# First chunk's scores of a fused attention and MoE kernel: one row for the cumulated gates against a product with a selection matrix

## The chip, the cores and the metric

The kernel runs on one core of a Trainium2 chip. The metric is the device time of one execution in microseconds (us), as the median of several runs. An engine is named PE (TensorE, matmuls), PEld (its weight loads), DVE (VectorE), ACT (ScalarE), POOL (GpSimd) or SP (SyncE, which issues most DMAs).

## What is computed

Attention with a decay from cumulated gates, then a mixture of four experts, then a gated MLP, all in float32 on 1152 tokens of width 512.

```python
B, H, S, D = 2, 8, 576, 64
scores = q @ k.T / sqrt(D)
cum = cumsum(log(clip(f, 1e-4, 1)))
scores = where(causal, -1e9, scores + cum[query] - cum[key])
x = softmax(scores) @ v
out = sum_e p[e] * (relu(x @ w1[e]) @ w2[e])
h = out @ w_in
y = (h * sigmoid(1.702 * h)) @ w_out
```

The term cum[query] is the same for all keys of a row and falls out of the softmax; only cum[key] is added.

## The kernel before

The tokens are four chunks: of each of the two batches its first 256 and its last 320. Attention is done chunk by chunk, and as soon as a chunk is ready the expert layers on it are put between the attention steps of later chunks, so that PE always has matmuls. After attention the expert and MLP layers run over three wide chunks of 384 tokens. Numbers in the layers are split in a high and a low part of type float32r, and three products of one pass each stand for one float32 product. `w_pairs` holds the weight loads, `due` and `need` say how many attention steps (`pull`) go between two layer groups, and the framework's scheduler then decides the order of each engine's instructions.

Attention goes by units. For each unit there are stages in a software pipeline: scores (PE, line 394), mask and row maximum (DVE, L420), exponential with row sum (ACT, L434), division by the sum (DVE L440 and L441, POOL L443), transposition (PE L461, copied out by ACT L53 or DVE L468), product with v (PE L491). The scores go to two buffers in PSUM (`ps_s`), so PE may write the scores of a tile only when DVE has read the tile two before it.

Chunk 0, the first 256 tokens of batch 0, is the one that `plain` names. It has no high and low parts: its score products are float32 products, which the chip runs as two passes. A unit of it is one head with two query tiles, one of 128 queries by 128 keys and one of 128 by 256. Eight heads make eight units.

For these, `load_plain` (L293) loads for four heads at a time k (`kd`) and q (`qd`) transposed, 64 partitions each, and v (`vd`). A 65th row is added: ones times 1/NEG in `qd` (a POOL memset, L304, NEG is -1/8), and the cumulated gates in `kd`, which `load_plain_rest` (L306) brings by two DMAs that ACT issues (L310) when the first half of the gates is cumulated. The product over 65 rows then holds the scores and the gates.

The gates themselves: `fr` is loaded, clipped (DVE L657), its logarithm taken (ACT L658), summed along the row (DVE L659), each in two halves of 256 and 320 columns. Then `cumd` is written to DRAM (L665, issued by ACT) for the later chunks, which read it back as rows spread over partitions (`cb`, `cbs`). For the later chunks q and k of a head pair stand on two halves of 64 partitions (`load_heads`, L320), and POOL splits them (`prep_parts`, L50 and L333).

```python
qd, kd, vd = groups[h0]
nc.scalar.dma_start(out=kd[64:65], in_=cum[h0:h0 + G, :wk])
for g in range(G):
    heads[0, h0 + g] = dict(vd=vd[:, :, g, :], qd=qd[:65, g], kd=kd[:65, g])
```

## Time and profile before

| | us |
|---|---|
| median of 3 runs | 737.25 |
| lowest and highest run | 737.0, 743.86 |
| the profiled execution | 737.77 |
| its span in the trace | 736.1 |
| PE busy | 715.6 |
| POOL busy | 277.6 |

All times in the trace count from the start of the span. The profiled execution has 1.7 us around its span. PE is busy for 97% of the span, but matmuls are pipelined, so that its records overlap; a busy PE is not a PE at its peak.

### The profile page before, as it was taken

To read this page: it belongs to the slowest core of one execution; us is meant where nothing else is said; L and a number is where in the kernel's file an instruction comes from. 1 tells how busy PE (TensorE), PEld (TensorE's weight loads), DVE (VectorE), ACT (ScalarE), POOL (GpSimd) and SP (SyncE) were. 2 spreads that over 40 slices of the span, in tenths; PEclk is the share of its full clock that TensorE was granted. 3 is DMA by queue.
4 is the path that set the end of the run, shared out by engine and by line. 5 is a ranking of instruction groups with operands and counts; after the bars stand their busy time and mean duration, and the time that the engine had idled before them with its cause. 6 is when DMAs were issued, how large, how long until landed. Compare 5 with 4: busy or idle time off the path is not lost.

```text
span 736.1 us, 11924 instructions
## 1 busy us (share of the span) xinstructions
PE 715.6 (97%) x4488; PEld 674.9 (92%) x4488; DVE 460.2 (63%) x1023; ACT 268.4 (36%) x629; POOL 277.6 (38%) x345
## 2 busy tenths in 40 slices
PE   4999999999999999999999999999999999999998
PEld 3576788888899999999998999999999999999997
DVE  4785666575758999999999633445972124424422
ACT  4564554566542233222211221223354433323420
POOL 4886974653432022233232433232462222222220
PEclk9999999999999999999999999999999999999999
DMA  8776534332216464464443301000100000000012
GB/s 290 222 233 208 159 123 132 90 103 86 73 51 216 144 194 149 148 183 117 130 144 115 86 24 35 1 1 1 58 0 1 1 1 1 1 0 1 1 44 86
DMA packets 29496, 67.23 MB, mean 91 GB/s; under 512 B 3032, under 2 KB 4576, under 8 KB 29440
## 3 DMA queue, kind: packets, MB, share of 16 engines
q1 hardware_dynamic: 29392, 66.44, 28.9%
q8 instruction: 35, 0.57, 0.3%
q14 instruction: 21, 0.17, 0.1%
q10 hardware_dynamic: 48, 0.05, 0.0%
HBM read 64.05 MB, written 2.41 MB: 90 GB/s over the span
## 4 chain that ended last, share of the span: by engine, by line
PE 75%; DVE 13%; DMA 5%; issue 3%; POOL 3%; ACT 0%; ACTq 0%; DVEq 0%; POOLq 0%
PE m L604 32%; PE m L560 31%; PE s L394 5%; PE t L461 3%; PE x L491 3%; DVE wlo L163 3%; DMA mst<-in_wa_mlp_dram 2%; DMA mst<-in_wb_mlp_dram 2%; DVE cvd L226 1%; DVE wf L220 1%; DVE cvt L214 1%; DVE tmp L618 1%; DVE cvt L212 1%; DVE hl L587 1%; DVE wf L228 1%
## 5 line engine op out<-in xcount | busy, mean ns | idle before, releaser
L620 POOL TENSOR_TENSOR acc<-acc,tmp 128x384 f32<-128x384 f32 (+3 forms) x112 | 111.2, 1004 | 248.9 <-DVE tmp L618 238.0
L604 PE MATMUL m<-hh,wlo 128*128 128x384 f32 (+2 forms) x640 | 128.0, 320 | 1.4 <-DVE wlo L163 1.3
L604 PE MATMUL m<-hh,whi 128*128 128x384 f32 (+2 forms) x640 | 129.1, 321 | 0.0
L604 PE MATMUL m<-hl,whi 128*128 128x384 f32 (+2 forms) x640 | 127.7, 320 | 0.0
L560 PE MATMUL m<-xh,whi 128*128 128x384 f32 (+2 forms) x624 | 126.1, 322 | 0.4 <-DVE hl L587 0.2
L560 PE MATMUL m<-xl,whi 128*128 128x384 f32 (+2 forms) x624 | 126.2, 321 | 0.0
L560 PE MATMUL m<-xh,wlo 128*128 128x384 f32 (+2 forms) x624 | 126.2, 321 | 0.0
L53 ACT ACTIVATE whi<-wst 128x512 fp32r<-128x512 f32 x103 | 64.9, 631 | 119.8 <-PE m L560 58.0
L163 DVE TENSOR_TENSOR wlo<-wst,whi 128x512 fp32r<-128x512 f32 x112 | 93.3, 836 | 24.3 <-ACT whi L53 13.7
L604 PEld LDWEIGHTS m<-hh,wlo 128*128 128x128 f32 x640 | 105.6, 188 | 3.2 <-DVE wlo L163 2.4
L604 PEld LDWEIGHTS m<-hh,whi 128*128 128x128 f32 x640 | 105.8, 188 | 1.7 <-issue 0.7
L560 PEld LDWEIGHTS m<-xh,whi 128*128 128x128 f32 x624 | 103.1, 188 | 3.7 <-issue 1.7
L604 PEld LDWEIGHTS m<-hl,whi 128*128 128x128 f32 x640 | 105.9, 188 | 0.8 <-issue 0.5
L560 PEld LDWEIGHTS m<-xl,whi 128*128 128x128 f32 x624 | 103.8, 188 | 0.9 <-issue 0.7
L560 PEld LDWEIGHTS m<-xh,wlo 128*128 128x128 f32 x624 | 103.7, 188 | 1.1 <-issue 1.0
L595 POOL TENSOR_TENSOR hl<-tmp,hh 128x384 fp32r<-128x384 f32 x48 | 49.1, 1025 | 133.3 <-ACT hh L53 133.3
L586 ACT ACTIVATE hh<-m 128x384 fp32r<-128x384 f32 (+2 forms) x112 | 48.9, 436 | 117.5 <-PE m L560 117.5
L587 DVE SCALAR_TENSOR_TENSOR hl<-m,hh 128x384 fp32r<-128x384 f32 (+2 forms) x112 | 54.9, 493 | 34.9 <-ACT hh L586 34.9
L618 DVE TENSOR_TENSOR tmp<-m,dpb 128x384 f32<-128x384 f32 (+2 forms) x80 | 40.9, 512 | 38.4 <-PE m L604 32.0
L593 DVE TENSOR_TENSOR tmp<-m,sg 128x384 f32<-128x384 f32 x48 | 26.6, 554 | 54.2 <-ACT sg L592 54.2
L443 POOL TENSOR_SCALAR e<-e,sm 128x128 f32<-128x128 f32 (+4 forms) x72 | 47.4, 668 | 29.4 <-DVE sm L441 15.7
L434 ACT ACTIVATE e<-e,mx 128x128 f32<-128x128 f32 (+4 forms) x72 | 41.9, 583 | 35.9 <-DVE mx L420 34.9
(80 smaller groups left out, 742.6 us busy)
## 6 DMA issues: line engine op xcount, KB each, us to landing
wst<-in_wa_moe_dram SPq DMA_DIRECT2D x28, 512.0 KB, 3.5
wst<-in_wb_moe_dram SPq DMA_DIRECT2D x28, 512.0 KB, 3.8
mst<-in_wa_mlp_dram SPq DMA_DIRECT2D x16, 512.0 KB, 3.5
mst<-in_wb_mlp_dram SPq DMA_DIRECT2D x16, 512.0 KB, 3.6
cb<-cumd SPq DMA_DIRECT2D x16, 256.0 KB, 4.1
vd<-in_vp_dram SPq DMA_DIRECT2D x8, 320.0 KB, 13.1
kq<-in_qk_dram SPq DMA_DIRECT2D x4, 608.0 KB, 7.2
cbs<-cumd SPq DMA_DIRECT2D x8, 288.0 KB
```

What stands on the lines that cost most here:

```text
L53: nc.scalar.activation(out=out, in_=in_, func=AF.Copy)
L163: sub = nc.vector.tensor_sub(lf, raw, f(hf))
L394: nc.tensor.matmul(pt[:, :z - a], lhsT=lr[i][0], rhs=lr[i][1], start=i == 0, stop=i == n - 1)
L434: nc.scalar.activation(out=e[:, off:off + w], in_=e[:, off:off + w], func=AF.Exp, scale=-1.0, bias=mx, accum_out=sm[:, 0, k:k + 1])
L443: nc.gpsimd.tensor_scalar(out=e[:, off:off + w], in0=e[:, off:off + w], scalar1=sm[:, 0, i:i + 1], scalar2=1.0, op0=ALU.mult, op1=ALU.mult)
L560: nc.tensor.matmul(p[:, :n], lhsT=w[:, k, :], rhs=x[c][:, k, :], start=(j == 0 and k == 0), stop=(j == 2 and k == 3))
L586: nc.scalar.activation(out=hh[:, g, :n], in_=p[:, :n], func=AF.Relu)
L587: nc.vector.scalar_tensor_tensor(out=hl[:, g, :n], in0=p[:, :n], scalar=0.0, in1=f(hh[:, g, :n]), op0=ALU.max, op1=ALU.subtract)
L595: nc.gpsimd.tensor_sub(hl[:, g, :n], t[:, :n], f(hh[:, g, :n]))
L604: nc.tensor.matmul(p[:, :n], lhsT=w[:, k, :], rhs=x[:, k, :n], start=(j == 0 and k == 0), stop=(j == 2 and k == 3))
L618: nc.vector.tensor_mul(t[:, :n], p[:, :n], d)
L620: nc.gpsimd.tensor_add(a, a, t[:, z])
```

## The change

q and k of a head pair of chunk 0 now stand on two row halves of one tile (`kq0`, 64 rows a head), loaded with 128 partitions. The 65th row, its memsets and the two DMAs that ACT issued are gone. Each score tile is the sum of two products in PSUM: first one float32r product of a selection matrix with the gates, then the float32 product of q and k over 64 rows. `cum_hl` holds the high part of the gates of all 16 rows (batch and head) in partitions 0 to 15 and the low part in 64 to 79, zero between; `sel[:80, h]` is 1/NEG in the rows h and 64 + h and zero elsewhere. ACT rounds the high part, DVE takes the difference, POOL makes the zeros and the selection matrix. A unit of chunk 0 is now a head pair with one query tile, as in the other chunks: 128 by 128 for both heads, then 128 by 256 for both heads; there are still eight units.

```diff
--- before.py
+++ after.py
@@ -291,25 +291,14 @@
 
         return c == 0
 
-    def load_plain(h0):
-        G, wk = 4, SA
-        qd, kd = ((h_p.tile([128, 4 * WN], F32, tag=t, name=n) if h0 else
-                   kq_p.tile([128, S + QW], F32, tag="kq", name=n))[:, :G * wk].rearrange("p (g s) -> p g s", g=G)
-                  for n, t in (("qd", "hh"), ("kd", "hl")))
-        vd = v_p.tile([128, 2 * G * D], F32, tag="vd0", name="vd", bufs=2).rearrange("p (t g d) -> p t g d", t=2, g=G)
-        for i, t in enumerate((kd, qd)):
-            nc.sync.dma_start(out=t[0:64], in_=qk0[h0 // G, i].rearrange("d (g s) -> d g s", g=G))
-        nc.sync.dma_start(out=vd, in_=v0[h0 // G].rearrange("p (t g d) -> p t g d", t=2, g=G))
-
-        nc.gpsimd.memset(qd[64:65], 1.0 / NEG)
-        groups[h0] = (qd, kd, vd)
-
-    def load_plain_rest(h0):
-        G, wk = 4, SA
-        qd, kd, vd = groups[h0]
-        nc.scalar.dma_start(out=kd[64:65], in_=cum[h0:h0 + G, :wk])
-        for g in range(G):
-            heads[0, h0 + g] = dict(vd=vd[:, :, g, :], qd=qd[:65, g], kd=kd[:65, g])
+    def load_plain(k):
+
+        t = kq_p.tile([128, S + QW], F32, tag="kq", name="kq0")[:, :4 * SA].rearrange("p (g s) -> p g s", g=2)
+        vd = v_p.tile([128, 8 * D], F32, tag="vd0", name="vd", bufs=2).rearrange("p (t g d) -> p t g d", t=2, g=4)
+        nc.sync.dma_start(out=t, in_=qk0[2 * k:2 * k + 2].rearrange("g p s -> p g s"))
+        nc.sync.dma_start(out=vd, in_=v0[k].rearrange("p (t g d) -> p t g d", t=2, g=4))
+        for g in range(2):
+            groups[4 * k + 2 * g] = (t[:, g], vd[:, :, 2 * g:2 * g + 2, :])
 
     def load_heads(p, h0):
 
@@ -356,8 +345,6 @@
 
     def units_of(c, h0):
 
-        if plain(c):
-            return [(c, ((h,), (0, 128))) for h in (h0, h0 + 1)]
         _, s0, n = CH[c]
         return [(c, ((h0, h0 + 1), (q0,))) for q0 in range(s0, s0 + n, 128)]
 
@@ -372,8 +359,10 @@
         for q0 in tiles:
             w = min(q0 + 128, S)
             if plain(c):
-                st = heads[c, hs[0]]
-                mm = [(0, w, [(st["qd"][:, q0:q0 + 128], st["kd"][:, :w])])]
+
+                kq = groups[hs[0]][0]
+                mm = [(0, w, [(sel[:80, h, :], cum_hl[:80, :w]), (kq[r, SA + q0:SA + q0 + 128], kq[r, :w])])
+                      for h, r in zip(hs, (slice(0, 64), slice(64, 128)))]
             else:
                 p = pass_of[c]
                 hi, lo = (pairs[p, hs[0]][k] for k in ("hi", "lo"))
@@ -484,7 +473,7 @@
             for g in range(2):
                 ph = ph_of[c, h - 1 + g]
                 if plain(c):
-                    lhsT = heads[c, h - 1 + g]["vd"][:, i, :]
+                    lhsT = groups[h - 1][1][:, i, g, :]
                 else:
                     lhsT = pairs[pass_of[c], h - 1]["vd"][:, i, g, :]
                 rhs = ph[:, i, o:n] if i < 4 else ph[:, 3, 0:64]
@@ -644,7 +633,16 @@
 
     nc.scalar.activation(out=cum[:, :1], in_=ones[:, :1], func=AF.Ln)
     load_plain(0)
-    load_plain(4)
+    load_plain(1)
+
+    cum_hl = h_p.tile([128, 4 * WN], F32R, tag="hh", name="cumhl")[:, :SA]
+    sel = h_p.tile([128, 4 * WN], F32R, tag="hl", name="sel")[:, :8 * 128].rearrange("p (h q) -> p h q", h=8)
+    nc.gpsimd.memset(f(cum_hl)[:80], 0.0)
+    round_pool(cum_hl[:80], f(cum_hl)[:80])
+    nc.gpsimd.memset(f(sel)[:80], 1.0 / NEG)
+    for a, z in ((0, 64), (64, 80)):
+        nc.gpsimd.affine_select(out=sel[a:z], in_=f(sel)[a:z], pattern=[[-1, 8], [0, 128]], compare_op=ALU.is_equal,
+                                fill=0.0, base=0, channel_multiplier=1)
     nc.gpsimd.memset(mask, 0.0)
     nc.gpsimd.affine_select(out=mask[:, 128:], in_=mask[:, 128:], pattern=[[-1, 128]],
                             compare_op=ALU.is_ge, fill=-1e10, base=0, channel_multiplier=1)
@@ -659,8 +657,8 @@
         nc.vector.tensor_tensor_scan(out=cum[:, a:z], data0=ones[:, a:z], data1=fr[:, a:z],
                                      initial=cum[:, a - 1:a] if a else 0.0, op0=ALU.mult, op1=ALU.add)
         if a == 0:
-            load_plain_rest(0)
-            load_plain_rest(4)
+            round_act(cum_hl[:16], cum[:, :SA])
+            nc.vector.tensor_sub(cum_hl[64:80], cum[:, :SA], f(cum_hl[:16]))
     nc.vector.tensor_scalar(out=fr, in0=cum, scalar1=1.0 / NEG, scalar2=None, op0=ALU.mult)
     nc.scalar.dma_start(out=cumd, in_=fr)
     load_heads(passes[1], 0)
@@ -758,8 +756,7 @@
 
     def first(k, q):
 
-        a = np.stack([k[0, :, :SA], q[0, :, :SA]]).reshape(2, 2, 4, SA, D)
-        return a.transpose(1, 0, 4, 2, 3).reshape(2, 2, D, 4 * SA)
+        return np.concatenate([a[0, :, :SA].transpose(0, 2, 1).reshape(4, 2 * D, SA) for a in (k, q)], axis=-1)
 
     def pairs(k, q, s0):
```

Of before, the first rows of PE: `kd` and `qd` are the 65-row operands, `s` a score tile in PSUM, `t` a transposition.

```order
L394 MATMUL s_175<-kd_131,qd_130 128x128 [waits DMAHW2_49,DMAHW5_49,DMAHW1_49,Pool_49]
L394 MATMUL s_177<-kd_131,qd_130 128x256
L394 MATMUL s_191<-kd_131,qd_130 128x128 [waits DVE_49]
L394 MATMUL s_193<-kd_131,qd_130 128x256 [waits DVE_49]
L394 MATMUL s_215<-kd_131,qd_130 128x128 [waits DVE_49]
L461 MATMUL t_202<-identr_124,e_179 128x128 [waits Pool_49]
```

Of the changed kernel, the same place of PE.

```order
L383 MATMUL s_176<-cumhl_138,sel_139 128x128 [waits DVE_49,Pool_49]
L383 MATMUL s_177<-cumhl_138,sel_139 128x128
L383 MATMUL s_176<-kq0_130 128x128 [waits DMAHW1_49]
L383 MATMUL s_177<-kq0_130 128x128
L383 MATMUL s_194<-cumhl_138,sel_139 128x256 [waits DVE_49]
L383 MATMUL s_194<-kq0_130 128x256
L383 MATMUL s_195<-cumhl_138,sel_139 128x256 [waits DVE_49]
L383 MATMUL s_195<-kq0_130 128x256
L450 MATMUL t_208<-identr_124,e_182 128x128 [waits Pool_49]
```

The first matmul waited for three DMAs and POOL; it now waits for DVE (the gates) and POOL (the selection matrix), and the DMA is waited for by the third. Two score tiles of a pair stand side by side only in the first unit; later each tile has its selection product just ahead of it.

On POOL, the start of the kernel before: `qd` are the ones of the 65th row, `ones_126` the mask, `e_179` the first unit's exponentials, `khi` and `klo` the parts of the next chunk's first head pair.

```order
L648 MEMSET ones_126 128x256
L304 MEMSET qd_137 1x1024 [waits Pool_49]
L651 MEMSET identr_124 128x128 [waits Pool_49]
L649 ISA
L649 AFFINE_SELECT ones_126<-ones_126 128x128
L304 MEMSET qd_130 1x1024 [waits Pool_49]
L652 AFFINE_SELECT identr_124<-identr_124 128x128 [waits Pool_49]
L50 TENSOR_SCALAR tri_123<-ones_126 128x128
L443 TENSOR_SCALAR e_179<-e_179,sm_180 128x128 [waits DVE_49,Activation_49]
```

And of the changed kernel.

```order
L646 MEMSET ones_126 128x256
L640 MEMSET cumhl_138 80x256
L642 MEMSET sel_139 80x1024
L649 MEMSET identr_124 128x128
L647 ISA
L647 AFFINE_SELECT ones_126<-ones_126 128x128 [waits Pool_49]
L50 TENSOR_SCALAR cumhl_138<-cumhl_138 80x256 [waits Pool_49]
L644 AFFINE_SELECT sel_139<-sel_139 64x1024 [waits Pool_49]
L644 AFFINE_SELECT sel_139<-sel_139 16x1024 [waits Pool_49]
L650 AFFINE_SELECT identr_124<-identr_124 128x128 [waits Pool_49]
L50 TENSOR_SCALAR tri_123<-ones_126 128x128
```

Two memsets of 1024 columns are gone; a memset of 256, a memset of 1024, a rounding and two selects of 1024 columns stand ahead of the identity.

On ACT, before: the two DMAs of the gates stand ahead of the one to `cumd` and of the load of the exponential's table.

```order
L658 ACTIVATE fr_125<-fr_125 16x320 [waits DVE_49]
L310 DMA kd_131<-fr_125 1x4x256 [waits DVE_49]
L310 DMA kd_138<-fr_125 1x4x256
L665 DMA cumd_110<-fr_125 16x576 [waits DMAHW1_49,DVE_49,Activation_49]
L434 ACT_TABLE_LOAD
```

And of the changed kernel.

```order
L656 ACTIVATE fr_125<-fr_125 16x320 [waits DVE_49]
L53 ACTIVATE cumhl_138<-fr_125 16x256 [waits DVE_49,Pool_49]
L663 DMA cumd_110<-fr_125 16x576 [waits DMAHW1_49,DVE_49,Activation_49]
L423 ACT_TABLE_LOAD
```

The rounding of the gates took the place of the two DMAs.

## Rows read from the trace of the kernel before

**Rows 1.** The page: busy time, share of the span and instructions of each engine.

```profile
PE 715.6 (97%) x4488; PEld 674.9 (92%) x4488; DVE 460.2 (63%) x1023; ACT 268.4 (36%) x629; POOL 277.6 (38%) x345
```

**Rows 2.** Chain that ended last, 8 to 24 us: start, us, what.

```profile
by line: PE s L394 44.0%; DMA cumd<-fr 21.0%; PE x L491 15.7%; PE t L461 14.2%; DVE wlo L163 7.8%; DVE e L420 3.6%; issue 1.9%; DVE ph L468 1.6%; DVE sm L441 1.0%; DVE dps L263 0.7%; DVE mx L420 0.2%
...
6.65 3.36 DMA cumd<-fr
...
10.13 1.63 PE s L394 x4
...
12.27 1.65 PE s L394 x4
...
20.61 1.47 PE x L491 x5
```

**Rows 3.** Timeline, first microseconds: start, us, engine, line, operation [idle before <-releaser].

```profile
0.80 0.31 POOL L648 MEMSET ones<- 128x256 f32 x1 [0.29 <-POOLq L785]
...
1.17 0.95 POOL L304 MEMSET qd<- 1x1024 f32 x1
...
2.17 0.21 POOL L651 MEMSET identr<- 128x128 f32 x1
2.42 0.29 POOL L649 TENSOR_SCALAR_AFFINE_SELECT ones<-ones 128x128 f32<-128x128 f32 x1
...
3.89 1.78 DVE L659 TENSOR_TENSOR_SCAN fr<-ones,fr 16x256 f32<-16x256 f32 x2
...
4.72 1.81 ACTq L310 DMA_DIRECT2D kd<-fr  x2
5.71 0.45 DVE L664 TENSOR_SCALAR fr<-fr 16x576 f32<-16x576 f32 x1
...
7.05 1.28 ACT L434 ACT_TABLE_LOAD   x1 [2.58 <-DVE fr L664]
...
11.26 0.40 ACT L434 ACTIVATE e<-e,mx 128x128 f32<-128x128 f32 x1 [2.93 <-DVE mx L420]
```

**Rows 4.** DMA issues: count, KB each, median us from issue to landing.

```profile
kd<-in_qk_dram SPq DMA_DIRECT2D x2, 256.0 KB, 3.6
qd<-in_qk_dram SPq DMA_DIRECT2D x2, 256.0 KB, 4.2
```

**Rows 5.** Stretches: busy time of PE, PEld, DVE, ACT, POOL, granted clock, DMA share, GB/s.

```profile
2.00:6.00 4.00, 0.00 (x0) 0.00 (x0) 3.24 (x5) 1.17 (x4) 2.56 (x6) 1.00 0.86 203
...
10.00:14.00 4.00, 3.77 (x11) 2.84 (x11) 1.83 (x11) 1.48 (x7) 0.57 (x2) 1.00 1.04 405
...
38.00:42.00 4.00, 3.11 (x17) 1.71 (x17) 2.71 (x6) 0.48 (x2) 4.00 (x7) 1.00 0.55 210
...
80.00:200.00 120.00, 118.80 (x841) 100.50 (x841) 79.27 (x240) 67.11 (x185) 68.59 (x94) 1.00 0.35 107
```

**Rows 6.** Groups of PE instructions by form, 10 to 21.9 us: busy, mean ns.

```profile
L394 PE MATMUL s<-kd,qd 65*128 65x256 f32 x10 | 5.7, 676 | 0.1
```

**Rows 7.** Groups of PE instructions by form, 22 to 31 us.

```profile
L394 PE MATMUL s<-kd,qd 65*128 65x256 f32 x6 | 1.9, 397 | 0.0
```

**Rows 8.** Timeline, score passes and weight loads of PE (merged neighbours).

```profile
15.25 1.02 PEld L394 LDWEIGHTS s<-kd,qd 65*128 65x128 f32 x4
...
15.46 1.95 PE L394 MATMUL s<-kd,qd 65*128 65x128 f32 x6
```

**Rows 9.** Line 394: weight loads of the 65-row products, ns least/median/most, first and last start.

```profile
L394 PEld LDWEIGHTS s<-kd,qd x32: 186/288/337, 10.1 to 27.3; 65*128 65x128 f32 x32
```

**Rows 10.** Chain that ended last: a run of float32r layer products of 256 columns.

```profile
45.62 2.40 PE m L581 x20
```

**Rows 11.** Who waited for whom, 10 to 24 us: total us, times, longest.

```profile
PEld s L394 <- DVE mx L420: 1.2, 4, 0.4
```

**Rows 12.** Groups of POOL instructions by form, 10 to 50 us: busy, mean ns.

```profile
L333 POOL TENSOR_TENSOR klo<-kq,khi 128x576 fp32r<-128x576 f32 x3 | 4.3, 1418 | 0.1
...
L443 POOL TENSOR_SCALAR e<-e,sm 128x256 f32<-128x256 f32 x8 | 3.8, 476 | 0.0
```

## Prediction

> **What bounds the kernel now.** I first read the busy shares. PE is busy for 97% of the span [rows 1], so an edit pays through PE: where it starts earlier, where it waits less, or by the work it is given. The change touches only the start, so the chain of waits from 8 to 24 us came next [rows 2]: up to 10.0 us a DMA ends the wait, then PE's first score product runs at 10.13, and from there PE's own products of chunk 0 (scores, transpositions, products with v) make up most of the chain, with DVE in between. The chain names the DMA to `cumd`, but the first matmul does not read `cumd`; what it reads is the gate row in `kd`. The DMAs for that row are issued by ACT from 4.72 to 6.53, just ahead of the one named [rows 3], while k and q have landed about 3.6 and 4.2 us after their issue [rows 4], so I put the wait down to the two small gate DMAs, queued behind the loads.
>
> Next I compared stretches [rows 5]: PE idles ahead of 10.13 and a little around 38 to 42, and from 80 to 200 us it is busy for 118.80 of 120. So an earlier start can carry to the end if chunk 0 itself ends earlier, since PE afterwards works off a fixed amount. The loads of the first microseconds move 203 GB/s, those from 10 to 14 us 405.
>
> Last, the score passes by form: a pass of 256 columns takes 676 ns before 21.9 us [rows 6] and 397 after 22 [rows 7]. The granted-clock column reads 1.00 in both, but the durations fit the level of 1.2 GHz first and 2.4 GHz after, with chunk 0's products nearly back to back between 12 and 22 us.
>
> **The change part by part.** The sum is made against the profiled execution, 737.77 us (736.1 of span and 1.7 around it); it stands 0.5 above the median of 737.25, and a shift in us is carried over to the median unchanged.
>
> The wait for the gate row goes. What is late next? There are three candidates.
>
> First, q and k. The same 512 KB come in one load for the first four heads. Before, the second half landed at 1.87 + 4.2 = 6.1 us. If 128 partitions give the 405 GB/s of the later stretch instead of 203, it is about 1.3 us of transfer less, near 4.8. Either way this is not after 6.2, and it is only waited for by the third matmul.
>
> Second, the gates on DVE. The two halves of the sum end at 3.89 + 1.78 = 5.67 us. The rounding on ACT lies beside the second half. The difference over 256 columns follows it on DVE; its nearest row is the scaling of 576 columns with 0.45, so 0.2 to 0.45, taken as 0.3. The low part is there at 6.0.
>
> Third, the selection matrix on POOL, in the order shown above. From the rows [rows 3]: the mask 0.31 us from 0.80, a memset of 256 columns 0.31, one of 1024 columns 0.95, the identity 0.21, a select of 128 columns 0.29; that is near 2.95 with the gaps. The rounding of 80x256 is like a POOL scaling of 256 columns, 0.48 [rows 12]. Then come two selects of 1024 columns, for which there is no row: a memset grows from 0.21 to 0.95 between 128 and 1024 columns, 4.5 times, so a select of 0.29 becomes 1.3; ends are 1.0 (like a memset) and 2.3 (eight times 0.29). I take 1.3, by the nearest growth seen: 3.45 + 2.6 = 6.05, with ends 5.5 and 8.1. So the first matmul moves from 10.13 to about 6.2, and the **gain at the start is 3.9 us**, with ends 4.1 (DVE binds) and 2.0 (POOL at 8.1).
>
> The first exponential ran at 11.26. ACT must load its table first, which before followed 0.9 us after the scaled gates were done at 6.16. Now DVE does the difference ahead of that scaling, and the table is loaded by about 8.1; PE does not wait for the exponentials in its first units, so I cost this at nothing. If PE's cover went, the gain would be capped at 3.1.
>
> The added work is 16 selection products on PE: eight of 128 columns and eight of 256. Float32r products of 256 columns run at 2.40 us for 20 [rows 10], 0.12 each at 2.4 GHz, so 0.24 at 1.2. For 128 columns take the halves, 0.06 and 0.12 (they could cost as much as 256). Chunk 0 starts 3.9 us earlier and meets the same products, so I leave the clock's rise at the same distance after the first matmul. Then five of eight units, six products of 128 and four of 256, run at the low level: 6 x 0.12 + 4 x 0.24 = 1.7 us, and the other six 2 x 0.06 + 4 x 0.12 = 0.6. Together **2.3 us**. Bounds: if they fit into PE's waits for DVE (1.2 us of them stand in this stretch [rows 11]) and the high level comes early, as little as 0.3; if all cost what a whole pass does at the low level (half of 0.427 and 0.427, as six passes of 1024 columns take 1.95 with their tail [rows 8]), 8 x 0.21 + 8 x 0.43 = 5.1.
>
> Here a rule of the Trainium skill speaks against the change. The row first: the weight loads of the 65-row products take 288 ns in the median [rows 9], and yet six passes, each with its own load, stand within 1.95 us [rows 8], which is what their columns need. The page "TensorE: Matmul & The Clock Gate", Part 3, under "The mechanism", says that weight loads run beside matmuls in flight only when their row groups differ (though it also names a background weight buffer). The selection product uses rows 0 to 79 and thus meets both head halves, so by the rule alone the 16 added loads would be exposed; by the row they are hidden. I go by the row; the other is a rival below.
>
> The score products lose one row (64 for 65) and keep their two passes and columns: nothing. Two heads' products side by side on row halves occur only in the first unit, worth at most one tile of 128 columns, 0.43 us; taken as nothing. The unit's shape changes (two heads, one tile), but masks, exponentials, divisions and copies keep their number and total width: nothing. On POOL four operations that split the next chunk's q and k now stand together between the first and the second unit's divisions, some 4 us by two `klo` at 1.4 and 1.2 and two `khi`; before it was three of the four. The second unit's transpositions queue behind them. PE has the scores of units 2 and 3 to do meanwhile, some 4 us at the low level, so this too is hidden; uncovered it would cost about 1 us. On SP the later loads go out sooner, as six loads become four.
>
> The sum: -3.9 + 2.3 = -1.6 us. That makes 736.2 for the profiled execution and **735.7** for the median.
>
> **The rivals.** (A) The selection products are nearly free, as chunk 0 is in truth paced by DVE, ACT and POOL, which do no more than before, and by loads that come faster. For: PE waits for DVE at scores, and POOL is full around 38 to 42 while PE idles [rows 5]. Against: from 12 to 22 us the chain is nearly all PE [rows 2]. Then -3.9 + 0.3 = -3.6, that is 733.7.
>
> (B) The clock rises sooner, as the products now stand denser. The low level now lasts from 10.13 to some 22, 12 us, with more than 10 of them filled; half of it, 6 us, at the high level would save 3. On top of the forecast: 732.7. Against: PE was already without gaps there before it rose.
>
> (C) Slower: each selection product, standing ahead of its tile's score product on the same rows, costs its weight load too. The price is 16 times 0.29 [rows 9], 4.6, plus the 2.3: -3.9 + 6.9 = +3.0, that is 740.3. This decides once a selection product costs more than 3.9 / 16 = 0.24 us, exposed. Against it stands the gapless run of passes [rows 8]. It is the rule named above.
>
> (D) The earlier start is taken back: chunk 0 ends earlier, but the next chunk's attention waits for POOL or for `cb` as before, so it ends as before: 737.3. For: POOL is at its full 4.00 us between 38 and 42. Against: POOL's own work there starts earlier too, and PE is busy before and after.
>
> (E) A different order from the scheduler makes or closes a gap of PE in the attention stages, either sign, with no place I can name.
>
> **How the numbers follow.** Forecast 0.40; A 0.20, B 0.12, C 0.10, D 0.12, E 0.06. What a measurement of this kernel can tell from no change is about 1%, 7.4 us: the bounds are 729.9 and 744.6. None of the cases with a price reaches them; A and B together (-6.6, 730.7) come near, and E could pass either. So faster 0.06, same 0.89, slower 0.05. The range goes from somewhat below B to C's price with a little room removed: 731.5 to 740.0; below it lie A and B together and part of E, above it C's worst and part of E. The forecast's own ends are start 2.0 with products 3.3 (+1.3, 738.6) and start 4.1 with products 1.0 (-3.1, 734.2).
>
> **What would show each step.** Right: the first matmul near 6.2 us, released by POOL or DVE and no longer by a DMA; the selects of 1024 columns near 1.3 us; the first exponential near 8.1; stretches of the first 10 us with more than 203 GB/s; the selection products 0.1 to 0.25 us apart from what follows; chunk 0's last score product (near 27.3 before) 1 to 2 us earlier, and the same shift at 80 us. Wrong: a first matmul after 8 us; a shift that is gone by 80 us (D); a score stage that takes longer by over 4 us (C); a change of clock level well before 18 us (B).

## The result, and the profile after

The changed kernel takes 742.28 us (median of 22 runs, 740.51 to 746.09), the kernel before 737.17 on the same chip (22 runs, 735.32 to 743.86). The ratio is 1.0052, with an interval from 1.0035 to 1.0068: some 4 us slower by the ratio and 5 by the medians, where 1.6 us faster was forecast, and outside the range. The profiled execution took 742.74 us with a span of 740.9, 4.8 more than the span before. (The profiled executions of two experiments below, the first zeroed row and the last run, were disturbed ones of 2,439 and 996 us; of these only the other runs' times are used.)

The page of the changed kernel, as [rows 1]:

```profile
PE 723.9 (98%) x4504; PEld 680.2 (92%) x4504; DVE 459.4 (62%) x1024; ACT 269.1 (36%) x630; POOL 277.8 (37%) x348
```

PE has 16 instructions more and is busy for 8.3 us more; their columns alone are 1.3 us at 2.4 GHz.

The timeline of its first microseconds (start, us, engine, line), as [rows 3]:

```profile
3.16 2.59 POOL L644 TENSOR_SCALAR_AFFINE_SELECT sel<-sel 64x1024 fp32r<-64x1024 f32 x2
3.42 3.00 DVE L657 TENSOR_TENSOR_SCAN fr<-ones,fr 16x256 f32<-16x256 f32 x2
...
6.45 0.42 DVE L661 TENSOR_TENSOR cumhl<-fr,cumhl 16x256 fp32r<-16x256 f32 x1
...
7.01 0.66 PE L383 MATMUL s<-cumhl,sel 80*128 80x128 f32 x2 [7.01 <-DVE cumhl L661]
7.60 0.80 PE L383 MATMUL s<-kq 64*128 64x128 f32 x4
7.81 1.28 ACT L423 ACT_TABLE_LOAD   x1 [2.44 <-DVE fr L662]
...
9.11 0.40 ACT L423 ACTIVATE e<-e,mx 128x128 f32<-128x128 f32 x1
```

The first matmul came 3.1 us earlier, at 7.01, and DVE released it: the two scans (the running sums of the gates) took 3.00 us where they had taken 1.78. The selects took 1.3 us each, and no DMA is waited for. So the edit does what it says at the start.

Next the score products of the first chunk, timeline of PE, and below it that of PEld (the weight loads) for the same time:

```profile
8.79 0.58 PE L383 MATMUL s<-cumhl,sel 80*128 80x256 f32 x1 [0.39 <-DVE mx L409]
9.30 1.22 PE L383 MATMUL s<-kq 64*128 64x256 f32 x2
10.44 0.58 PE L383 MATMUL s<-cumhl,sel 80*128 80x256 f32 x1
10.95 1.22 PE L383 MATMUL s<-kq 64*128 64x256 f32 x2
12.10 0.47 PE L450 MATMUL t<-identr,e 128*128 128x128 f32 x1
```

```profile
9.30 0.50 PEld L383 LDWEIGHTS s<-kq 64*128 64x128 f32 x2 [0.23 <-issue]
10.44 0.28 PEld L383 LDWEIGHTS s<-cumhl,sel 80*128 80x128 f32 x1 [0.65 <-DVE sm L430]
10.95 0.50 PEld L383 LDWEIGHTS s<-kq 64*128 64x128 f32 x2 [0.22 <-issue]
```

Read the starts. From 8.79 to 9.30 a selection product holds PE for 0.51 us, though its 256 columns need 0.21 at 1.2 GHz; the load of the next weights starts only at 9.30, with the product that uses it. The two passes of a head then take 1.14 us until the next load may start. One tile is 1.66 us (8.79 to 10.44). Before, six passes of 1024 columns took 1.95 with the tail [rows 8], 0.85 for a tile of two passes of 256. Loads that were hidden behind the pass ahead of them now stand in the open.

The chain from 8 to 24 us, as [rows 2]:

```profile
by line: PE s L383 69.5%; PE t L450 16.7%; PE x L480 15.7%; DVE e L409 1.7%; issue 0.3%; DVE mx L409 0.1%
...
13.82 5.28 PE s L383 x12
```

Scores have grown from 44.0% to 69.5% of it. The stretches, as [rows 5], with one more from 80 to 90 us:

```profile
2.00:6.00 4.00, 0.00 (x0) 0.00 (x0) 3.20 (x4) 1.58 (x5) 3.82 (x7) 1.00 0.87 293
10.00:14.00 4.00, 4.00 (x12) 2.22 (x10) 1.72 (x10) 1.51 (x6) 3.44 (x6) 1.00 1.06 404
38.00:42.00 4.00, 4.00 (x22) 2.37 (x21) 2.74 (x12) 0.84 (x3) 1.52 (x3) 1.00 1.00 295
80.00:90.00 10.00, 7.35 (x59) 6.53 (x57) 3.86 (x10) 2.97 (x6) 10.00 (x12) 1.00 0.31 112
80.00:200.00 120.00, 116.30 (x827) 97.59 (x826) 75.55 (x244) 68.24 (x189) 69.41 (x98) 1.00 0.35 110
```

From 80 to 90 us PE is idle for 2.65 of 10 us while POOL is busy for all of them; from 80 to 200 it had been idle for 1.2 before, and is for 3.7 now.

To see where time goes, I worked out one number from all PE rows of each trace: the time so far less what the columns started so far need at 2.4 GHz. (A pass of a float32 product counts its columns twice, as at one clock it takes about twice the time of a float32r product of the same width [rows 8, rows 10]. The columns of selection and unused products don't count, so their time is in the number as a loss.) It grows where PE waits, where loads are exposed and where the clock is low. In us, for the kernel before in two executions, the changed one, and two experiments told below:

```
at us                     10    34    42    80    90   730
before                  10.0  20.2  23.7  28.3  28.9  82.6
before, again            9.9  23.2  26.4  29.1  31.6  83.9
changed                  9.1  25.5  28.9  30.9  34.5  87.1
changed, adjacent        9.1  21.8  26.5  32.7  35.6  89.0
changed, cbs in two      9.1  25.5  26.9  27.6  28.9  81.2
```

The first two rows are the same program in the same order of PE, so they differ by the execution alone, and what is seen to differ is the clock. The trace's record of the clock at 2.4 GHz begins at 21.96 us in the first execution before, at 36.99 in the second, and at 40.17 in the changed kernel. So the changed kernel is compared with the second: 0.8 ahead at 10 us, 2.3 behind at 34, 1.8 at 80, 2.9 at 90, 3.2 at the end. Chunk 0's last score pass starts at 36.0 us, where it was at 27.5 in the first execution before and at 29.9 in the second.

### The profile page after: what moved, and what is told of

The parts are those of the page before. It is cut to its first block, busy times and chain, and to the rows that moved or that the text cites. A ratio compares the mean times of both kernels' runs of the same rounds, so it can differ in the third digit from the quotient of the medians.

```text
span 740.9 us, 11958 instructions
## 1 busy us (share of the span) xinstructions
PE 723.9 (98%) x4504; PEld 680.2 (92%) x4504; DVE 459.4 (62%) x1024; ACT 269.1 (36%) x630; POOL 277.8 (37%) x348
## 4 chain that ended last, share of the span: by engine, by line
PE 78%; DVE 11%; issue 3%; POOL 3%; DMA 3%; ACT 1%; POOLq 0%; DVEq 0%; ACTq 0%
PE m L593 34%; PE m L549 33%; PE s L383 6%; PE t L450 3%; PE x L480 3%; DVE wlo L163 2%; DMA mst<-in_wa_mlp_dram 2%; DVE cvd L226 1%; POOL e L432 1%; DVE wf L220 1%; DVE hl L576 1%; DVE cvt L214 1%; DVE tmp L607 1%; DVE cvt L212 1%; DVE wf L228 1%
## 5 line engine op out<-in xcount | busy, mean ns | idle before, releaser
L593 PE MATMUL m<-hl,whi 128*128 128x384 f32 (+2 forms) x640 | 129.2, 320 | 0.0
L163 DVE TENSOR_TENSOR wlo<-wst,whi 128x512 fp32r<-128x512 f32 x112 | 92.2, 824 | 30.7 <-ACT whi L53 15.6
L432 POOL TENSOR_SCALAR e<-e,sm 128x128 f32<-128x128 f32 (+4 forms) x72 | 45.2, 638 | 40.4 <-DVE sm L430 26.5
```

Of the source, the lines that this page charges most:

```text
L163: sub = nc.vector.tensor_sub(lf, raw, f(hf))
L432: nc.gpsimd.tensor_scalar(out=e[:, off:off + w], in0=e[:, off:off + w], scalar1=sm[:, 0, i:i + 1], scalar2=1.0, op0=ALU.mult, op1=ALU.mult)
L593: nc.tensor.matmul(p[:, :n], lhsT=w[:, k, :], rhs=x[:, k, :n], start=(j == 0 and k == 0), stop=(j == 2 and k == 3))
```

## The experiments

Four theories. Theory 1: the products and their exposed loads are the cost. Theory 2: any early edit makes the scheduler redraw the order of all engines, and the new order has other gaps. Theory 3: the clock, which rises late or falls back when PE has gaps. Theory 4, formed on the way: the next chunk's start is held by a transfer. The expectations were written as the theories grew, so their numbers differ from these at places (4 is the clock in some of them); each says in words which theory it means. A ratio is always to the kernel before on the same chip, while times of different experiments can come from different chips.

**The start without the products.** In the kernel before, the gate row is zeroed by POOL instead of filled by ACT's two DMAs, so the gates are left out of chunk 0; then the same with 64 rows; then the changed kernel without its selection products (also without gates).

```diff
+        nc.gpsimd.memset(kd[64:65], 0.0)
-        nc.scalar.dma_start(out=kd[64:65], in_=cum[h0:h0 + G, :wk])
```

> The kernel before with the gate row of chunk 0 set to zero by a POOL memset instead of loaded by the two DMAs that ACT issues (the gates are left out of chunk 0's scores). 65-row products as before, nothing added on PE. All theories: the first matmul comes when k and q have landed, near 6.2 us instead of 10.1. What an earlier start alone is worth: if it carries to the end, 737.2 - 3 to 4 = 733 to 734; if it is taken back on the way, 736 to 737.

> As e1_row65_zero, but the products take 64 rows instead of 65 (the zero row is not read; the gates are left out of chunk 0's scores). Theory 1 (products on a row half expose their weight loads): passes of 256 columns start 0.59 and 0.56 us apart at the low clock instead of 0.43, those of 128 columns 0.37 and 0.35 instead of 0.21, the high clock comes later than 22 us, and the time is 2 to 5 us above e1_row65_zero. Theory 2 (the number of added products is the cost) and theory 3 (the scheduler's order and POOL): same as e1_row65_zero within 1 us.

> The changed kernel without the product with the selection matrix (the gates are left out of chunk 0's scores). Theory 1: the switch between 80-row and 64-row products is gone, but passes on one row half still expose their loads where the other half does not stand beside them; tile of 256 columns 0.6 to 1.15 us a head at the low clock instead of 1.66; time 735 to 738. Theory 2: back to the forecast's start gain, 733 to 735. Theory 3: still near 741, as the order of units and POOL's work are those of the changed kernel.

> The same kernel as e1_row65_zero once more, for a profile of a common execution, as the one taken had no high clock at all (span 2437 us). Theory 4: the profile shows the high level coming near 40 us or later, and the time is again 740 to 744, though nothing was added on PE and only the start moved. Theory 1: a high level near 18 to 22 us and 733 to 737, the first result being an accident.

Measured: the zeroed row 743.0 (ratio 1.0073, 1.005 to 1.0096), repeated 741.13 (1.0051, 1.0029 to 1.0072); 64 rows 736.1 (0.9997, 0.9979 to 1.0015); no selection 739.97 (1.0043, 1.0028 to 1.0058). The zeroed row keeps the products of before, starts them 3.6 us earlier, and loses 4 us all the same. One row less gives 5 us back, with no work changed that could: but some 1,000 of PE's 4,488 rows stand in another order. So an earlier start by itself brings nothing, and an order with gaps costs as much as the whole change. Leaving the selection products out of the changed kernel gives back 2.3 us by the medians and 0.7 by the ratios, whose intervals overlap: the added work is not the bulk of the loss. Who waits for whom on PE, 22 to 92 us (us in total, times, longest), in the kernel before and then in the repeated run:

```profile
PE t L461 <- POOL e L443: 0.8, 2, 0.5
```

```profile
PE t L461 <- POOL e L443: 5.9, 3, 2.6
```

With 64 rows there is none, although POOL waits about as long for loads of `cb` and `cbs` (12.1 us against 13.6, from 12 to 92 us): a late POOL need not cost PE anything; it depends on what PE's order has to put in meanwhile. The kernel with 64 rows stays at 1.2 GHz up to 40.63 us and is none the slower: a late clock alone isn't the loss either. (In the repeated run the clock rose at 19.64 us and was back at 1.2 GHz from 29.88 to 46.95.)

The run with 64 rows also tells what exposes a load. Its PE timeline, with the same place of the kernel before first:

```profile
10.13 3.79 PE L394 MATMUL s<-kd,qd 65*128 65x128 f32 x10 [10.13 <-DMA cumd<-fr]
```

```profile
6.56 3.79 PE L394 MATMUL s<-kd,qd 64*128 64x128 f32 x10 [6.56 <-DMA qd<-in_qk_dram]
10.29 0.48 PE L461 MATMUL t<-identr,e 128*128 128x128 f32 x1
10.70 1.22 PE L394 MATMUL s<-kd,qd 64*128 64x256 f32 x2
11.85 0.47 PE L461 MATMUL t<-identr,e 128*128 128x128 f32 x1
```

Ten passes of 64 rows in a row take 3.79 us, as ten of 65 rows do. Two of them between transpositions of 128 rows take 1.15 us, as long as between the selection products of the changed kernel. From a pass of 256 columns to a transposition at 1.2 GHz it is 0.56 us with 64 rows, all five times in this trace, and 0.43 with 65 in the kernel before. So it is not the 64 rows by themselves that expose a load, but the step between them and a product on more rows. Theory 1 expected such loads here and a time above that of the zeroed row; the loads are there, and the time is 5 us below.

**Products in program order.** Both selection products first, then both heads, kept so:

```diff
-                    nc.tensor.matmul(pt[:, :z - a], lhsT=lr[i][0], ...)
+                    m = nc.tensor.matmul(pt[:, :z - a], lhsT=lr[i][0], ...)
+                    if plain(c) and (i or pt is pts[1]):
+                        tc.keep_in_program_order(m)
```

> The changed kernel with chunk 0's four products of a unit kept in program order on PE: both selection products, then both 64-row products side by side on the two row halves. Theory 1: one switch a unit instead of two and the halves run beside each other, so a unit of 128 columns takes about 1.3 us and one of 256 about 1.9 at the low clock (now 2.2 and 3.3), chunk 0 ends up to 9 us earlier than in the changed kernel, and the time falls to 733 to 738. Theory 2: the products are as many as before, so 741 to 743. Theory 3: 740 to 743, since POOL and the loads are unchanged.

742.38 (1.0082, 1.0062 to 1.0102): no gain in time, though PE's order is that of the changed kernel but for 34 places, and its timeline shows what was wanted:

```profile
8.72 0.80 PE L383 MATMUL s<-cumhl,sel 80*128 80x256 f32 x2 [0.39 <-DVE mx L411]
9.45 1.23 PE L383 MATMUL s<-kq 64*128 64x256 f32 x4
10.92 0.83 PE L452 MATMUL t<-identr,e 128*128 128x128 f32 x2 [0.25 <-POOL e L434]
```

Four passes of two heads take 1.23 us, as long as the two passes of one head above: they run side by side on their row halves. Two tiles take about 2.0 us instead of 3.3. By 34 us this kernel is 3.7 ahead of the changed one (21.8 against 25.5 in the table), and by 80 us 1.8 behind. The timeline of POOL shows where:

```profile
47.86 0.45 POOL L335 TENSOR_TENSOR cb<-cb,tri 128x128 f32<-128x128 f32 x1 [7.13 <-DMA cb<-cumd]
```

And who waited on PE, 22 to 92 us:

```profile
PE t L452 <- POOL e L434: 6.4, 4, 2.6
```

POOL stands for 7.13 us at a load of `cb`, and its divisions `e` for the chunks at work queue behind. The clock fell back to 1.2 GHz as well, from 36.46 to 43.28 us and from 56.94 to 60.35; how the loss divides between the waits and the clock isn't shown.

**No row halves.** q padded with zeros to 128 rows, so that the passes of q and k take 128 rows and none a row half; 512 KB more are loaded.

```diff
-(kq[r, SA + q0:SA + q0 + 128], kq[r, :w])])
+(kq[1][:, r + q0:r + q0 + 128], kq[0][:, :w])])
```

> The changed kernel with q of each head of chunk 0 padded with zeros to all 128 rows (from the host, as the other chunks' last tiles have it), so that every product of chunk 0 uses the whole array and none a row half; the selection products stay. 512 KB more are loaded. Theory 1: weight loads are hidden again, a tile of 256 columns takes 1.07 us at the low clock instead of 1.66, one of 128 columns 0.53 instead of 1.11; chunk 0 ends 5 to 9 us earlier than in the changed kernel and the high clock comes before 30 us; 735 to 739. Theory 2 (the added products): as the changed kernel, 741 to 743. Theory 5 (the order that the scheduler makes of the attention stages decides, and any edit draws it anew): anything from 736 to 745 with chunk 0 faster, the difference arising after 40 us.

742.87 (1.0057, 1.0026 to 1.0088). Between products of 80 and of 128 rows no load is exposed: a tile of 256 columns takes 1.07 us, as expected, and not 1.66. Chunk 0's last score pass starts at 26.0, ten us before the changed kernel's, and nothing is gained. POOL and PE then:

```profile
33.70 0.70 POOL L347 TENSOR_TENSOR cbs<-cbs,tri 64x64 f32<-64x64 f32 x2 [3.92 <-DMA cbs<-cumd]
```

```profile
34.92 0.82 PE L453 MATMUL t<-identr,e 128*128 128x128 f32 x2 [2.75 <-POOL e L435]
```

POOL waits for `cbs` until 33.70, PE for POOL, and the clock is back at 1.2 GHz from 30.57 to 40.81. In this run and in the adjacent one, an early end of chunk 0 meets a transfer.

**The clock.** Unused float32 products ahead of the first score (7 in the changed kernel, 14 before), then with three more behind each unit's scores, and a later start by filling `sel` four times.

```diff
+    for _ in range(7):
+        nc.tensor.matmul(wp[:, :256], lhsT=wz[:, :128], rhs=wz, start=True, stop=True)
```

> The changed kernel with seven float32 products of a tile of ones (128 rows, 256 columns, result not used) put on PE ahead of chunk 0, while PE has nothing else to do. Theory 4 (the low clock, which in the changed kernel lasts from 7 to 40 us instead of from 10 to 22, is what costs the time): the high level comes near 7 us, chunk 0's tiles take half as long, chunk 0 ends 5 to 10 us earlier, and the time falls by 3 to 8, to 734 to 739, unless the level falls back. Theory 1 (exposed weight loads) alone: the loads stay exposed, gain of at most 2 us, 740 to 742. Theory 3 (order, POOL, loads): no gain, 741 to 743.

> The kernel before with fourteen such products on PE in the 8 us in which it waits for the gate row. Theory 4: the high level comes near 7 us instead of 22, some 12 us of chunk 0 run at it, and as chunk 0's passes fill PE there, up to 6 us are won, less what DVE, ACT and POOL then bind: 731 to 736. The other theories say nothing of it; 736 to 738 if PE's clock does not bound chunk 0.

> The kernel before, unchanged, for a second trace. If the clock's rise at 22 us is a property of the kernel, it comes between 18 and 26 us again; if it is a matter of chance from one execution to the next, it can come anywhere up to 45 us, with a span a few us longer.

> The changed kernel with the selection matrix filled four times over on POOL, so that the first matmul comes near 10.5 us as before the change; products, units and row halves are those of the changed kernel. Theory 1 and 2 (the products' cost): chunk 0 and the end come 3 to 4 us later than in the changed kernel, 745 to 746. Theory 4 (an earlier start is no gain, as it leaves PE short of work or at the low clock later): 740 to 743, no later than the changed kernel.

> The changed kernel with the seven unused products ahead of chunk 0 and three more (128 rows, 256 columns, float32) behind the scores of each unit of chunk 0, kept in their place on PE. They do no work for the result. Theory 4: the high clock comes near 5 us and does not fall in chunk 0, which then ends near 25 us in place of 36 although PE has 10 us of work more; 734 to 740. If the added work counts and the clock does not: 745 to 752.

> The kernel before with 14 unused float32 products ahead of the first score (they fit into the wait of PE up to 10.13 us) and three unused ones of 128 rows by 256 columns behind the scores of each unit of the first chunk, 24 in all, 10.3 us of PE work at 2.4 GHz. Theory 3 (the clock): PE has no gap in the first chunk, the clock rises by 16 us and stays up, unlike in the run that had the 14 products alone (758.0); the time is 736 to 741, 17 to 22 below that run although it does more. Theories 1 and 2: work is added on the path, 758.0 + 10.3 = 768, or at best 737 + 10 = 747.

> The changed kernel with the four products of a unit in program order (both selections, then both heads, as in the run of adjacent products), 7 unused products ahead and three behind each unit's scores. Theory 3 (the clock): high from about 13 us on and kept, 736 to 738.5 as the run with the filling alone (738.2). Theory 1: the exposed loads between a selection and a head product are halved in number, 8 x 0.3 = 2.4 us less at the high level: 735 to 736.5. Theory 2: another order again, 733 to 743.

Measured: 742.95 with 7 ahead (1.0072, 1.0046 to 1.0099); 757.97 before with 14 (1.0278, 1.0249 to 1.0306); the kernel before again 739.19 in one run; 752.36 with the later start (1.0179, 1.0125 to 1.0232), which neither expectation had: the first product came 2.7 us later, the time grew by 10; with filling 738.19 changed (0.999, 0.9956 to 1.0024), 745.62 before (1.0089, 1.0049 to 1.013) and 743.51 adjacent (1.0077, 1.0055 to 1.0099). That points to the clock as a cost: filling adds 13.2 us of products at 2.4 GHz to the changed kernel and takes 4 us off, and 12 off the kernel before with its 14. But filling isn't a gain over the kernel before, and it didn't keep the clock in any of the three traces: 1.2 GHz came back from 38.23 to 45.06 us in the changed kernel, twice for 3.4 us before, and from 35.13 to 41.96 adjacent, there after another wait of POOL for `cbs` (4.9 us). With the 7 ahead alone the clock was up from 4.67 to 11.50 us and then only from 42.22 on. With the 14 ahead alone it was back at 1.2 GHz for 41 us up to 102, PE waited 9.9 us for POOL's divisions from 22 to 92 us, and POOL 15.6 us for `cbs` from 12 to 92.

**The same order for both.** The scheduler's timing simulation switched off, so that the edit moves few instructions.

```diff
-    with tile.TileContext(nc, schedule_with_timeline_sim=True) as tc:
+    with tile.TileContext(nc, schedule_with_timeline_sim=False) as tc:
```

> The kernel before, with the scheduler's own timing simulation switched off: the order of all engines then follows the program more closely, and the same edit moves far fewer instructions (145 of some 1,200 rows of PE between this kernel and the next run, against nearly all of them up to the end of attention between the two kernels as they stand). By itself this run has no forecast that tells theories apart: 735 to 760 us, since the order is a poorer one or not. It is the base of the next run.

> The changed kernel with the same switch. Theory 1 (the products of selection and their exposed weight loads cost the time by themselves): 3 to 6 us above the run before this one, with the head start of 3.1 us gone by 25 us and no later place of loss. Theory 2 (the loss lies in the order that the scheduler redraws, in which PE runs short between 36 and 90 us): within 2 us of the run before this one, or below it. Theory 3 (the clock): whichever of the two falls back to 1.2 GHz or rises later is slower, by about half of the difference in low time.

766.57 before (1.0363, 1.0313 to 1.0414), 771.62 changed (1.0425, 1.0376 to 1.0473). The gap of 5 us is there again, in favour of theory 1, but the intervals overlap, and PE waits 25 and 20 us for POOL from 50 to 200 us. It settles little.

**The load of cbs.** What several runs had in common was a DMA. SP's timeline in the changed kernel:

```profile
16.59 0.65 SPq L341 DMA_DIRECT2D cbs<-cumd  x1
18.00 5.68 SPq L309 DMA_DIRECT2D kq<-in_qk_dram  x1
...
24.35 5.67 SPq L142 DMA_DIRECT2D wst<-in_wa_moe_dram  x2
```

SP, which had issued a load in some 0.4 us each, stands for 5.7 us at the first issue after the second `cbs`, and at the second of the two issues of 24.35 for 4.6. The kernel before has such a stand too, so the change did not make it:

```profile
18.48 6.22 SPq L320 DMA_DIRECT2D kq<-in_qk_dram  x1
```

A stretch of the changed kernel in between (the last two columns are the DMA share of 16 engines and GB/s):

```profile
21.50:23.50 2.00, 2.00 (x9) 0.94 (x7) 2.00 (x6) 0.77 (x3) 2.00 (x4) 1.00 0.14 55
```

0.14 of 16 engines are 2.2, at 55 GB/s; 288 KB at that rate are 5.4 us, an estimate for each `cbs`. Its source is written with a leading dimension of two. The Trainium skill says why that matters ("DMA: Bandwidth & Descriptors", under "Why a DMA increments its semaphore by 16 and not by 1"): the number of engines is the largest up to 16 that divides the slowest dimension of both sides, here two; the 0.14 agrees. So it was loaded in two pieces:

```diff
-        nc.sync.dma_start(out=st["cbs"], in_=cumd[r:r + 2, :].unsqueeze(1).to_broadcast([2, 64, S]))
         for g in range(2):
             z = slice(64 * g, 64 * g + 64)
+            nc.sync.dma_start(out=st["cbs"][z], in_=cumd[r + g:r + g + 1, :].to_broadcast([64, S]))
```

> The changed kernel with each load of cbs as two DMAs of 64 partitions in place of one with a leading dimension of two. Theory 4 (chunk 0's end meets a transfer: the one-piece load goes over about two of the 16 DMA engines, 288 KB at some 50 GB/s, 5.8 us each, two in a row ahead of the next chunk; SP stands 5.7 us at 18 us and again at 24 us, and POOL's divisions queue behind the cbs operation): the stretches of 46 to 60 GB/s between 18 and 36 us go, SP's two stands too, POOL waits under 1 us for cbs instead of 3.5, and the time falls by 2 to 5 us, to 737 to 740. Theories 1 and 3 (the products, the clock): chunk 0 itself is as slow as it was, so under 1 us: 741.5 to 743. Theory 2 (any redrawn order): 735 to 744 with no sign.

> The kernel before with the same two-piece load of cbs. Theory 4: POOL waits 7.0 us in all for cbs and cb up to 92 us in the second profile of this kernel (8 in the sum of cb and cbs in the first with 3.9), of which PE feels the part at 36 to 42 us (0.9 us idle): 1 to 3 us faster, 734 to 736. Theory 3: only if the clock keeps its place; a rise by 22 us as before. Theory 2: 735 to 744.

The changed kernel takes 737.73 (0.9996, 0.9972 to 1.002), 4.6 us less than before this edit by the medians and 4.1 by the ratios. Here theory 2 is out: PE's order is the same, row for row, and up to 34 us the two are alike (25.5 in the table). After it, a stretch of the changed kernel and those of this run:

```profile
36.00:40.00 4.00, 4.00 (x17) 2.58 (x17) 1.85 (x7) 0.79 (x4) 2.45 (x6) 1.00 0.68 181
```

```profile
24.00:28.00 4.00, 4.00 (x12) 2.25 (x11) 1.73 (x8) 1.36 (x5) 3.83 (x10) 1.00 0.63 50
...
36.00:40.00 4.00, 4.00 (x28) 2.90 (x28) 3.47 (x14) 2.18 (x8) 3.09 (x6) 1.00 0.92 289
80.00:90.00 10.00, 9.65 (x68) 7.98 (x68) 8.42 (x23) 6.72 (x21) 6.04 (x9) 1.00 0.56 189
```

The gap of 80 to 90 is gone, and from 36 to 40 PE starts 28 products instead of 17. From 22 to 92 us PE now waits 0.3 us in all, where the changed kernel waited 2.5 us for POOL's divisions and 1.2 for DVE. SP's two stands are gone too; only 24 to 28 us still move little. POOL's waits for DMAs from 12 to 92 us, changed and then in two pieces:

```profile
POOL cb L335 <- DMA cb<-cumd: 5.5, 2, 3.4
POOL cbs L344 <- DMA cbs<-cumd: 3.5, 2, 2.0
```

```profile
POOL cb L335 <- DMA cb<-cumd: 2.6, 2, 2.5
```

A part of the gain is the clock: the record of 2.4 GHz begins at 33.82 instead of 40.17, and the group of 256 columns, from 33.9 to 40 us, shows it (busy us and mean ns stand behind the bar; changed first):

```profile
L383 PE MATMUL s<-kq 64*128 64x256 f32 x4 | 2.4, 712 | 0.0
```

```profile
L383 PE MATMUL s<-kq 64*128 64x256 f32 x4 | 1.4, 434 | 0.0
```

6.35 us less at half speed are 3.2 us of columns; the table has 3.3 between the two at 80 us and 5.6 at 90. Whether the earlier rise comes from the edit is open, as the two traces differ in nothing of PE up to then, and the kernel before rose at 22 and at 37 us. Chance alone is unlikely for the gain as a whole: the 12 runs end at 740.97, where the 22 of the changed kernel begin (740.51).

The kernel before gains nothing from it: 738.42 (0.9998, 0.9974 to 1.0022). There the edit redraws the order (some 400 rows of PE differ), and the clock fell back from 35.29 to 42.12. Nor was there much to gain: in the second execution of the kernel before POOL waits 11.3 us for `cb` and `cbs` from 12 to 92 us, but PE waits 0.4 us in all from 22 to 92.

**Both together.** Adjacent products and `cbs` in two pieces.

> The changed kernel with both edits: the four products of a unit in program order, as in the run of adjacent products (742.4), and cbs loaded in two pieces (737.7 by itself). PE's order is that of the adjacent run but for two instructions. In that run PE was 3.7 us ahead of the changed kernel at 34 us and lost it between 48 and 56 us, where POOL waited 7.1 us for a DMA of cb and PE 6.4 us in all for POOL's divisions. Theory 4 (the exposed loads cost 3.7 us and the slow load of cbs hid that): the wait of 7.1 us shrinks to under 3, and the time is 733.5 to 735.5, below both kernels. Theory 3 (the clock falls back wherever chunk 0 ends early): a fall between 33 and 45 us and 737 to 740. If the wait for cb stays as it was, cb has another cause than cbs, and the time is 740 to 743.

735.35 (0.9948, 0.9919 to 0.9976), beside 737.90 of the kernel before: below both kernels, by 2.6 and 6.9 us, and inside the place that theory 4 expected. Its runs with the clock never back at 1.2 GHz were at 733.7 to 734.4. PE's order is that of the adjacent run but for two instructions, which by itself took 742.38; the load was worth 7.0 us there, or 9.9 by the ratios. A part of it is again the clock, whose mean grant was 0.988 to 0.993 in the four runs there and 0.990 to 1.0 here. And beside the run with the load alone (737.73), the adjacent products look worth 2.4 us, or 3.5 by the ratios, hidden before and paid once the transfer is out of the way; but the two intervals just overlap. How long POOL waits for `cb` here isn't shown.

## Why the prediction was wrong

- "The first matmul moves from 10.13 to about 6.2": 7.01, a gain of 3.1 instead of 3.9, inside the ends given (4.1 and 2.0). The selects were priced right at 1.3 us; the end that bound was DVE's, since two scans of 16 rows took 3.00 us and not 1.78. The first exponential came at 9.11, not 8.1, and cost nothing, as said. The loads moved 293 GB/s, not 405, and weren't waited for.
- "I leave the clock's rise at the same distance after the first matmul": it came 33 us after the first matmul instead of 12, and in the second execution of the kernel before 27 after. One profiled execution had been taken for a property of the kernel. With the rise not tied to the start, 3.1 us at 1.2 GHz are worth half at the end; the table shows 0.8 at 10 us, with the time of the first selection products counted as lost. By itself this step is small: the two executions of the kernel before, 15 us apart in the rise, differ by 1.4 us in their spans.
- "0.24 us" for a selection product of 256 columns at the low level, by the row that loads are hidden [rows 8]: 0.51. This is the term of the sum that failed. "64 for 65 rows: nothing" is right for passes that follow each other (3.79 us for ten of either) but not for these: the head products stand between products on more rows and take 0.57 a pass instead of 0.43 at 256 columns. The mechanism is that of rival C, which was set at 0.10. Its price was 6.9 us in all; the changed kernel lost 3.1 us of columns between 10 and 34 us against the execution with the same clock, 6.2 us of time at 1.2 GHz. The row that hid the loads came from products on the same 65 rows; here products on 80 and on 64 rows alternate. The rule of the Trainium skill that was put aside ("TensorE: Matmul & The Clock Gate", Part 3, "The mechanism": loads run beside matmuls only where row groups differ) said that the added loads would be exposed, as they are, and the side-by-side passes of the adjacent run agree with it too. The traces don't bear it out as a whole: passes on the same 64 or 65 rows follow each other in 0.43 us with their loads hidden, and so do products of 80 and 128 rows in the run without row halves. The prediction saw in the order that two tiles of a pair stand together only in the first unit, and valued that at one tile; it was the use of the row halves that the order had undone.
- "An earlier start can carry to the end", and D at 0.12: this step failed too, to a large part. Between 34 and 80 us the kernel before itself loses 8.1 us (20.2 to 28.3), of which the changed kernel with the load in two pieces loses 2.1. That run is 5.3 behind at 34 us and level by 80 and 90. The prediction had seen POOL full from 38 to 42 us, and named `cb` as what might hold the next chunk, but left the load of `cbs` unread.
- "A different order, either sign, with no place I can name" (E, 0.06): it had a place, POOL's in-order queue, in which the divisions of the chunk at work stand behind operations that wait for `cb` and `cbs`. One row of the operand more or less moved the time by 5 us, with 5.9 us of such waits of PE in the slower run and none in the faster.
- Four splits together on POOL "hidden": behind `khi` the weight loads of transpositions wait 0.7 us in all up to 36 us, so this stands. "Same" as the likeliest class stands too.

So the loss has two parts: products whose exposed loads cost about 3 us of columns at equal clock, as much as the earlier start gave, and an order in which a slow transfer and POOL behind it leave PE short up to 90 us. The runs show that taking the transfer away recovers 4.6 us with the products and PE's order unchanged; that setting the products side by side then gives 2.4 more is likely, not sure. What part of the first is the clock's earlier rise stays open, and why the clock rises when it does is not shown by any run.

## What to carry to other kernels

Products on two row halves paid here only where they stood next to each other in PE's final order, so read that order and keep it by hand if need be; a product on more rows between them exposed a weight load on each side. Before pricing an earlier start, find what holds the next stage and look at how many DMA engines its load uses: writing a broadcast with a leading dimension of two as two DMAs was worth 4.6 us where PE felt the wait, and nothing in the kernel before. And don't take the moment of the clock's rise from one execution.

## What was not expected of the hardware

- The same kernel rose to 2.4 GHz at 21.96 us in one execution and at 36.99 in another; the spans differ by 1.4 us only (736.1 and 737.5), as most of the loss fell into later waits.
- A DMA of 288 KB with a leading dimension of two moved 55 GB/s, and SP's next issue stood 5.7 us behind it; with the load in two pieces that stand was gone.
- Two scans of 16 rows took 3.00 us on DVE while POOL worked on its selects, and 1.78 in the kernel before, which has no such selects; that the one slowed the other wasn't tried.
- Four passes on two row halves took 1.23 us and two passes on one half 1.22. A step from 64 rows to 80 or 128, or back, exposed a weight load; steps between passes of the same 64 rows, or between 80 and 128, did not.
